# First mixture in groups of 4, 5 and 7 blocks: weight pace computed, odd partial sums on ScalarE and GpSimd, last Horner step in PSUM, scaled words in place

## The chip, the cores and the metric

The kernel runs on one core of a Trainium2 chip. Its metric is the time in microseconds (us) of one execution on the device, the median of several runs; lower is better. The core has five engines that run side by side and meet at semaphores: TensorE (PE in the profile; PEld is its weight load), VectorE (DVE), ScalarE (ACT), GpSimd (POOL) and SyncE (SP), which here only issues transfers. SBUF is the working memory, PSUM the small memory into which TensorE writes. GpSimd does not touch PSUM in this kernel.

## What is computed

Three stages run one after the other on 1536 tokens of width 512. The first is an attention with a mask by clusters, the second and the third are two wide layers ("mixtures"). The change is about the first mixture; the numbers below come from the reference, cut to this part.

```python
def _moe_ref(x, w_in, w_out, a, b):          # first mixture: d_model 512, d_ff 2048
    h = x @ w_in
    h2 = h * h
    h3 = h2 * h
    P = a[0] + a[1] * h + a[2] * h2 + a[3] * h3
    Q = 1.0 + np.abs(b[0]) * np.abs(h) + np.abs(b[1]) * h2
    g = P / (Q + 1e-06)
    return g @ w_out

def _moe2_ref(x, w_gate, w_val, w_out):      # second mixture: d_ff 1536
    g = x @ w_gate
    silu = g * (1.0 / (1.0 + np.exp(-g)))
    return (silu * (x @ w_val)) @ w_out
```

The weights reach the chip as 64-bit numbers. Each product is made from two float32 parts of every operand, a high and a low one, with three matmuls in place of one (high by high, high by low, low by high).

## The kernel before

**Tiles.** A mixture handles the tokens in three tiles `t` of 512 and the hidden width in blocks `f` of 128: 16 blocks in the first mixture, 12 in the second. One **unit** is a pair (t, f). For a unit of the first mixture, `first_half` lets TensorE make `h_ps` in a PSUM bank (12 matmuls, `product`, L600); the other engines turn it into `g`, high and low; and three loop turns later (`LH = 3`) `project` (L676) adds `g` times the block's output weights into the four PSUM banks of `acc` (12 matmuls more). Turn `n` of the loop at L733 gives TensorE the product of unit `n` and then the projection of unit `n - 3`. Four `h_ps` banks (`ps_h`) and four `acc` banks (`ps_a`) exist.

**The steps of a unit.** ScalarE writes `tq` and `tp` from `h_ps` (L617, L618). VectorE finishes the two polynomials: `tq` (L619), and Horner's steps for P on `tp` (L622, L623), all of which read `h_ps`. One turn later ScalarE makes the reciprocal `tr` (L628 to L630), VectorE the high part of g (L633), the product of g and Q (L636) and the rest (L639), and a further turn later GpSimd multiplies the rest by `tr` for the low part (L644). VectorE therefore has six instructions of 512 columns for each unit: L619, L622, L623, L633, L636, L639.

**Groups.** SBUF can't hold all 16 blocks with both their weights, so the blocks go in groups: for each group, all three token tiles, and for each tile all blocks of the group. In the first mixture the groups have 2, 4, 4, 3 and 3 blocks. When the last block of a group has been projected for a tile, `evac` empties the four banks: in the first group ScalarE copies them into the tile `part` (L688); in the later ones VectorE adds each bank to `part` (L694). After the last group `split_y` makes high and low parts of the sum for the second mixture (L707 on ScalarE, L708 on VectorE). In the second mixture the odd banks already go another way: ScalarE copies the bank to `ts` (L691) and GpSimd adds it to `part` (L692).

**Weights.** A block of weights arrives as `raw`, with 512 pairs of a low and a high 32-bit word in each partition, so the low and the high words lie at every second place. ScalarE scales the high words into the tile `u` (`block_shift`, L70). VectorE shifts `u` by three bits into `c` (L79) and adds the upper bits of the low words (L83); `c` is the weight as float32. ScalarE writes its high part (L91) and GpSimd its low part (L94) into one of 18 places. Two blocks belong to each `f` of the first mixture and three to each `f` of the second. The first nine blocks are converted during the attention; the others in the loop, by the list `until`, which spreads the blocks of the next group evenly over the turns of the current one.

**Order.** Nothing reorders the work: each engine runs its instructions as the code issues them. In a turn these are, past the matmuls: the sum of bank 0, the low part of g for the unit two turns back, the sum of bank 1, the polynomials of this unit, the sums of banks 2 and 3, the reciprocal of the unit before, `split_y`, the weight steps, and the quotient (L633 to L639) of the unit before.

## Time and profile before

| | us |
|---|---|
| median of 3 runs | 832.88 (832.59 to 833.62) |
| the profiled execution | 837.14 |
| its span in the trace | 835.4 |
| TensorE busy | 804.5 (96%) |
| VectorE busy | 614.6 (74%) |
| ScalarE busy | 449.8 (54%) |
| GpSimd busy | 311.7 (37%) |

The profiled execution is 4.26 us longer than the median, 0.5%. The attention lasts until about 250 us, the first mixture from there to about 527 us, the second until the end. Shares over the whole span mix these three; the rows below are therefore mostly of the first mixture. Matmuls overlap in the pipeline, so the length of one matmul says less than the time from one run of 12 to the next.

### The profile page before, as it was taken

How to read it: one execution, taken by the hardware profiler on the slowest of the kernel's cores; microseconds unless marked ns; L12 is line 12 of the kernel's file. 1: busy time of each engine (PE TensorE's matmuls, PEld its weight loads, DVE VectorE, ACT ScalarE, POOL GpSimd, SP SyncE). 2: the span in 40 equal slices, each digit the busy share in tenths (PEclk: the TensorE clock that was granted, in tenths of full speed). 3: DMA queues.
4: the chain of work that ended last, by engine and by line, in shares of the span. 5: the costliest groups of instructions: out<-in, count | busy, mean ns of one | idle time of the engine just before them, and what ended most of it. 6: DMA issues, size and time to landing. Idle time of an engine off the chain costs nothing.

```text
span 835.4 us, 11054 instructions
## 1 busy us (share of the span) xinstructions
PE 804.5 (96%) x3900; PEld 604.6 (72%) x3900; DVE 614.6 (74%) x929; ACT 449.8 (54%) x850; POOL 311.7 (37%) x274
## 2 busy tenths in 40 slices
PE   4999999999999999999998999999999999999997
PEld 3656566566557887778777777788888888888885
DVE  7777777687657999999999999974774655543344
ACT  5776776677766886766666567723432222221110
POOL 4565576477131343332343333321243332220121
PEclk8999999999999999999999999999999999999999
DMA  5265335533212212111121111112232212000003
GB/s 186 81 200 192 106 119 196 153 104 124 68 61 93 94 52 75 51 50 43 34 77 51 51 56 59 63 51 76 88 115 75 74 53 76 26 26 1 0 13 139
DMA packets 26551, 67.91 MB, mean 81 GB/s; under 512 B 4448, under 2 KB 9536, under 8 KB 26496
## 3 DMA queue, kind: packets, MB, share of 16 engines
q1 hardware_dynamic: 26496, 67.21, 24.5%
q8 instruction: 31, 0.51, 0.2%
q14 instruction: 24, 0.20, 0.1%
HBM read 59.48 MB, written 3.19 MB: 75 GB/s over the span
## 4 chain that ended last, share of the span: by engine, by line
PE 70%; DVE 22%; issue 3%; ACT 2%; DMA 1%; POOL 0%; DVEq 0%; POOLq 0%; ACTq 0%
PE h_ps L600 28%; PE acc L676 16%; PE o_ps L411 9%; PE t_ps L400 8%; PE s_ps L344 4%; PE s_ps L346 4%; DVE g L633 3%; DVE part L694 3%; DVE td L639 3%; DVE td L636 3%; DVE tq L619 2%; DVE tp L622 2%; DVE c L79 1%; DVE tp L623 1%; PE sim L277 1%
## 5 line engine op out<-in xcount | busy, mean ns | idle before, releaser
L600 PE MATMUL h_ps<-yhl,w 128*128 128x512 f32 x864 | 202.0, 389 | 0.0
L600 PEld LDWEIGHTS h_ps<-yhl,w 128*128 128x128 f32 x864 | 162.6, 188 | 33.9
L676 PE MATMUL acc<-g,w 128*128 128x512 f32 x576 | 146.2, 397 | 11.5 <-DVE part L694 6.8
L600 PE MATMUL h_ps<-xhl,w 128*128 128x512 f32 x576 | 138.7, 390 | 0.0
L676 PEld LDWEIGHTS acc<-g,w 128*128 128x128 f32 x576 | 106.9, 189 | 42.7 <-DVE part L694 10.7
L94 POOL TENSOR_TENSOR w<-c,w 128x512 fp32r<-128x512 f32 x68 | 93.1, 1371 | 109.7 <-ACT w L91 102.6
L600 PEld LDWEIGHTS h_ps<-xhl,w 128*128 128x128 f32 x576 | 107.9, 188 | 23.8 <-issue 1.2
L644 POOL TENSOR_TENSOR g<-td,tr 128x512 fp32r<-128x512 f32 x46 | 59.5, 1294 | 172.9 <-DVE td L639 146.9
L354 DVE TENSOR_REDUCE st<-s_ps 128x1 f32<-128x768 f32 x96 | 91.4, 953 | 30.5 <-PE s_ps L346 27.9
L405 ACT COPY pt<-t_ps 128x384 f32<-128x384 f32 x160 | 70.4, 483 | 64.6 <-PE t_ps L400 64.5
L694 DVE TENSOR_TENSOR part<-acc,part 128x512 f32<-128x512 f32 x74 | 48.6, 684 | 76.7 <-PE acc L676 76.6
L676 PE MATMUL acc<-w,g 128*128 128x512 f32 x432 | 103.3, 389 | 0.0
L400 PEld LDWEIGHTS t_ps<-ident,p 128*128 128x128 f32 x576 | 62.3, 142 | 54.6 <-issue 43.5
L676 PEld LDWEIGHTS acc<-w,g 128*128 128x128 f32 x432 | 81.1, 188 | 16.8
L362 ACT ACTIVATE p<-s_ps,st 128x768 f32<-128x768 f32 x96 | 87.6, 913 | 2.1 <-DVE st L354 1.2
L411 PE MATMUL o_ps<-pt,v 128*64 128x384 f32 x384 | 82.9, 514 | 2.0 <-DVE x L419 1.9
L400 PE MATMUL t_ps<-ident,p 128*128 128x128 f32 x576 | 84.7, 284 | 0.0
L691 ACT COPY ts<-acc 128x512 f32<-128x512 f32 x22 | 12.9, 588 | 111.5 <-PE acc L676 111.5
L692 POOL TENSOR_TENSOR part<-ts,part 128x512 f32<-128x512 f32 x22 | 30.2, 1393 | 111.9 <-ACT ts L691 111.9
L617 ACT ACTIVATE tq<-h_ps,babs 128x512 f32<-128x512 f32 x48 | 33.0, 688 | 68.7 <-PE h_ps L600 67.1
L344 PE MATMUL s_ps<-k,q 128*128 128x512 f32 x192 | 58.9, 388 | 1.8 <-ACT p L362 1.6
L661 ACT ACTIVATE sg<-h_ps 128x512 f32<-128x512 f32 x36 | 21.6, 601 | 67.6 <-PE h_ps L600 67.6
(101 smaller groups left out, 1075.6 us busy)
## 6 DMA issues: line engine op xcount, KB each, us to landing
raw<-w_in_dram SPq DMA_DIRECT2D x16, 512.0 KB
raw<-w_out_dram SPq DMA_DIRECT2D x16, 512.0 KB
raw<-w_gate_dram SPq DMA_DIRECT2D x12, 512.0 KB
raw<-w_val_dram SPq DMA_DIRECT2D x12, 512.0 KB
raw<-w_o_dram SPq DMA_DIRECT2D x12, 512.0 KB
xq<-q_t_dram SPq DMA_DIRECT2D x14, 384.0 KB
xk<-k_t_dram SPq DMA_DIRECT2D x14, 384.0 KB
sq<-q_s_dram SPq DMA_DIRECT2D x8, 384.0 KB
```

Of the source, the lines that this page charges most:

```text
L94: nc.gpsimd.tensor_tensor(out=w[:, 1, :], in0=t["c"], in1=r32(w[:, 0, :]), op=ALU.subtract)
L344: nc.tensor.matmul(s_ps[:, lo:hi], t["q1"][:, qs], t["k1"][:, lo:hi], start=True, stop=False)
L346: nc.tensor.matmul(s_ps[:, lo:hi], t["q2"][0:KM, qs], t["k2"][0:KM, lo:hi], start=False, stop=True)
L354: nc.vector.tensor_reduce(out=st[:, 0, k:k + 1], in_=live["s", b, hp, half, i, e], axis=AX.X, op=ALU.max, negate=True)
L362: nc.scalar.activation(out=p, in_=live.pop(("s", b, hp, half, i, e)), func=AF.Exp, bias=st[:, 0, k:k + 1], accum_out=st[:, 1, k:k + 1],)
L400: nc.tensor.transpose(t_ps[:, j, :], p[:, kb * P:(kb + 1) * P], ident)
L405: nc.scalar.copy(out=pt[:, ks, qc], in_=t_ps)
L411: nc.tensor.matmul(live["o", b, hp, half][e * D:(e + 1) * D, :], heads[b, 2 * hp + e]["v"][:, kb, :], live["pt", b, hp, half, e][:, kb, :] ...
L600: nc.tensor.matmul(h_ps, w[:, wi, cs], x[:, xi, cc, :], start=(n == 0), stop=(n == 3 * NCC - 1))
L644: spread.tensor_tensor(out=g[:, 1, :], in0=td, in1=tr, op=ALU.mult)
L676: nc.tensor.matmul(acc[c], lhs, rhs, start=(first and m == 0), stop=(last and m == 2))
L694: nc.vector.tensor_tensor(out=pt[:, c, :], in0=banks[c], in1=pt[:, c, :], op=ALU.add)
```

## The change

The diff, cut to what moves work:

```diff
     def block_shift(t):
-        t["u"] = pools["u"].tile([P, DM], F32, tag="u", name="u")
-        nc.scalar.activation(out=t["u"], in_=t["high"], func=AF.Prelu, scale=2.0**-112, alpha=2.0**32)
+        nc.scalar.activation(out=t["high"], in_=t["high"], func=AF.Prelu, scale=2.0**-112, alpha=2.0**32)
...
-        nc.vector.tensor_single_scalar(out=cb, in_=t["u"].bitcast(U32), scalar=3, op=ALU.logical_shift_left)
+        nc.vector.tensor_single_scalar(out=cb, in_=t["high"].bitcast(U32), scalar=3, op=ALU.logical_shift_left)
...
-    GROUPS = ((1, [2, 4, 4, 3, 3]), (2, [2, 2, 3, 3, 2]))
+    GROUPS = ((1, [4, 5, 7]), (2, [2, 2, 3, 3, 2]))
...
                 nc.vector.scalar_tensor_tensor(
-                    out=tp, in0=tp, scalar=coef[:, 1:2], in1=h_ps, op0=ALU.add, op1=ALU.mult
+                    out=h_ps, in0=tp, scalar=coef[:, 1:2], in1=h_ps, op0=ALU.add, op1=ALU.mult
                 )
...
-                    out=g[:, 0, :], in0=tp, scalar=coef[:, 0:1], in1=tr, op0=ALU.add, op1=ALU.mult
+                    out=g[:, 0, :], in0=h_ps, scalar=coef[:, 0:1], in1=tr, op0=ALU.add, op1=ALU.mult
...
-                    out=td, in0=tp, scalar=coef[:, 0:1], in1=td, op0=ALU.add, op1=ALU.subtract
+                    out=td, in0=h_ps, scalar=coef[:, 0:1], in1=td, op0=ALU.add, op1=ALU.subtract
...
-                elif layer == 2 and c % 2 == 1 and not (end and t == NTT - 1):
-                    ts = tmp_p.tile([P, T], F32, tag="ts", name="ts")
+                elif c % 2 == 1 and not (layer == 2 and end and t == NTT - 1):
+                    ts = tmp_p.tile([P, T], F32, tag="ts" if layer == 2 else "tl", name="ts")
                     nc.scalar.copy(out=ts, in_=banks[c])
                     nc.gpsimd.tensor_tensor(out=pt[:, c, :], in0=ts, in1=pt[:, c, :], op=ALU.add)
...
+        need = [used[key, f][0] - 2 for key, f, _ in loads]
+        free = [-1] * (WA + WX + WB) + [used[key, f][-1] + 1 for key, f, _ in loads]
+
+        pace = []
+        at = float(ready[0])
+        for n in range(len(seq)):
+            at += max(((b + 1 - at) / max(need[b] - n, 1) for b in range(int(at), len(loads))), default=0)
+            while free[min(int(at + 0.999), len(loads)) - 1] > n + 1:
+                at = int(at + 0.999) - 1
+            pace.append(min(int(at + 0.999), len(loads)))
...
-                want = c0 + -(-(c1 - c0) * (n + 1 - n0) // (n1 - n0))
+                want = pace[n]
```

The list `pace` says for each turn how many blocks shall be converted by then: fast enough that each is ready two turns ahead of its first use, and no faster than the 18 places come free. By the two lists, 3 blocks more are converted before the second mixture begins (32 after the first nine, where there were 29): two of them in turns 0 and 1, where there were none, and eight in turns 2 to 11, where there were seven. In turns 36 to 40 there are none, in turns 44 to 47 one in each. Fewer groups mean fewer ends of a group and tile in the first mixture: 9 where there were 15, so 36 sums of one bank where there were 60. Of these 36, 12 stay copies by ScalarE, 12 go to VectorE (48 before), and 12 take the way over ScalarE and GpSimd. The result of the third step of Horner's scheme stays in the `h_ps` bank until L638, one turn longer than the bank was held before. The copy `ts` takes a place of the tag "tl", which before held only `tp`. Past L66 the line numbers of the changed kernel are lower by one, as far as the steps named here are concerned.

What this moves, first on VectorE where a tile of a group ends in the middle of the first mixture. Before, a group of 4 blocks; the row L694 is a sum of one bank:

```order
L639 SCALAR_TENSOR_TENSOR td<-tp,coef,td 128x512
L694 TENSOR_TENSOR part<-acc,part 128x512 x2
L619 SCALAR_TENSOR_TENSOR tq<-tq,babs,h_ps 128x512
L622 TENSOR_TENSOR tp<-tp,h_ps 128x512
L623 SCALAR_TENSOR_TENSOR tp<-tp,coef,h_ps 128x512
L694 TENSOR_TENSOR part<-acc,part 128x512 x2
L79 TENSOR_SCALAR c<-u 128x512
L83 SCALAR_TENSOR_TENSOR c<-raw,c 128x512
L633 SCALAR_TENSOR_TENSOR g<-tp,coef,tr 128x512
```

And VectorE in the changed kernel at such an end (group of 5 blocks):

```order
L638 SCALAR_TENSOR_TENSOR td<-h_ps,coef,td 128x512
L693 TENSOR_TENSOR part<-acc,part 128x512
L618 SCALAR_TENSOR_TENSOR tq<-tq,babs,h_ps 128x512
L621 TENSOR_TENSOR tp<-tp,h_ps 128x512
L622 SCALAR_TENSOR_TENSOR h_ps<-tp,coef,h_ps 128x512
L693 TENSOR_TENSOR part<-acc,part 128x512
L78 TENSOR_SCALAR c<-raw 128x512
L82 SCALAR_TENSOR_TENSOR c<-raw,c 128x512
L632 SCALAR_TENSOR_TENSOR g<-h_ps,coef,tr 128x512
```

Two of the four sums have left VectorE here, one ahead of the polynomials and one behind them; the shift of the weights reads `raw` itself, and the quotient reads the PSUM bank.

ScalarE at such a place, before (L617 and L618 are the first steps of a unit, L628 to L630 the reciprocal of the unit before, L70 and L91 the weights):

```order
L617 ACTIVATE tq<-h_ps,babs 128x512
L618 ACTIVATE tp<-h_ps,coef 128x512
L628 ACTIVATE tq<-tq 128x512
L629 ACTIVATE tr<-tq,cbias 128x512
L630 ACTIVATE tr<-tr 128x512
L70 ACTIVATE u<-raw 128x512
```

And ScalarE in the changed kernel:

```order
L690 COPY ts<-acc 128x512
L616 ACTIVATE tq<-h_ps,babs 128x512
L617 ACTIVATE tp<-h_ps,coef 128x512
L690 COPY ts<-acc 128x512
L627 ACTIVATE tq<-tq 128x512
L628 ACTIVATE tr<-tq,cbias 128x512
L629 ACTIVATE tr<-tr 128x512
L69 ACTIVATE raw<-raw 128x512
L90 CAST w<-c 128x512
```

The copy of bank 1 now stands ahead of the unit's first step, and the copy of bank 3 ahead of the reciprocal of the unit before.

## Rows read from the trace of the kernel before

**Rows 1.** Stretches: length, busy us (count) of PE, PEld, DVE, ACT, POOL; clock; DMA.

```profile
460.00:500.00 40.00, 37.64 (x163) 29.84 (x162) 38.70 (x59) 25.58 (x41) 14.05 (x11) 1.00 0.16 54
...
580.00:620.00 40.00, 40.00 (x179) 33.10 (x178) 24.00 (x33) 15.44 (x28) 12.16 (x8) 1.00 0.24 79
```

**Rows 2.** Chain of work that ended last, by time: start us, us, what.

```profile
290.93 2.72 PE h_ps L600 x12
293.65 2.72 PE acc L676 x12
...
388.95 1.20 DVE part L694 x2
...
411.76 1.20 DVE part L694 x2
...
471.74 1.20 DVE part L694 x2
...
489.77 1.20 DVE part L694 x2
```

**Rows 3.** Timeline, TensorE, third product and first of second mixture: start us, us, what.

```profile
260.22 5.75 PE L600 MATMUL h_ps<-xhl,w 128*128 128x512 f32 x24
...
523.75 3.83 PE L676 MATMUL acc<-g,w 128*128 128x512 f32 x10 [1.78 <-POOL g L644]
...
527.37 5.97 PE L600 MATMUL h_ps<-yhl,w 128*128 128x512 f32 x24
```

**Rows 4.** Timeline, VectorE, one unit with a weight block.

```profile
355.85 0.74 DVE L619 SCALAR_TENSOR_TENSOR tq<-tq,babs,h_ps 128x512 f32<-128x512 f32 x1
...
357.88 0.42 DVE L79 TENSOR_SCALAR c<-u 128x512 uint32<-128x512 uint32 x1
...
358.95 0.75 DVE L633 SCALAR_TENSOR_TENSOR g<-tp,coef,tr 128x512 fp32r<-128x512 f32 x1
...
361.20 0.74 DVE L619 SCALAR_TENSOR_TENSOR tq<-tq,babs,h_ps 128x512 f32<-128x512 f32 x1
```

**Rows 5.** VectorE's groups by line, 250 to 530 us: count, busy us, mean ns.

```profile
L633 DVE SCALAR_TENSOR_TENSOR g<-tp,coef,tr 128x512 fp32r<-128x512 f32 x46 | 39.9, 867 | 1.5 <-ACT tr L630 1.5
...
L694 DVE TENSOR_TENSOR part<-acc,part 128x512 f32<-128x512 f32 x42 | 26.9, 683 | 0.0
...
L79 DVE TENSOR_SCALAR c<-u 128x512 uint32<-128x512 uint32 x29 | 17.2, 592 | 0.0
L708 DVE TENSOR_TENSOR yhl<-part,yhl 128x512 fp32r<-128x512 f32 x4 | 2.5, 686 | 0.0
```

**Rows 6.** One line's instructions, whole run: duration ns least/median/most, first and last start.

```profile
L633 DVE SCALAR_TENSOR_TENSOR g<-tp,coef,tr x48: 739/747/1315, 257.5 to 539.8; 128x512 fp32r<-128x512 f32 x48
L79 DVE TENSOR_SCALAR c<-u x68: 414/420/1053, 65.3 to 762.5; 128x512 uint32<-128x512 uint32 x68
L622 DVE TENSOR_TENSOR tp<-tp,h_ps x48: 679/680/685, 255.3 to 530.0; 128x512 f32<-128x512 f32 x48
L83 DVE SCALAR_TENSOR_TENSOR c<-raw,c x68: 680/693/1757, 68.8 to 762.9; 128x512 uint32<-128x512 uint32 x68
```

**Rows 7.** Timeline: GpSimd's low part of a weight block, and VectorE beside it.

```profile
362.70 1.29 POOL L94 TENSOR_TENSOR w<-c,w 128x512 fp32r<-128x512 f32 x1
...
363.25 1.30 DVE L633 SCALAR_TENSOR_TENSOR g<-tp,coef,tr 128x512 fp32r<-128x512 f32 x1
```

**Rows 8.** The page, costliest groups: the sum over two engines in the second mixture.

```profile
L691 ACT COPY ts<-acc 128x512 f32<-128x512 f32 x22 | 12.9, 588 | 111.5 <-PE acc L676 111.5
L692 POOL TENSOR_TENSOR part<-ts,part 128x512 f32<-128x512 f32 x22 | 30.2, 1393 | 111.9 <-ACT ts L691 111.9
```

**Rows 9.** Groups by line of the whole run: scaling of the high words.

```profile
L70 ACT ACTIVATE u<-raw 128x512 f32<-128x512 f32 x68 | 45.3, 666 | 13.3 <-DMA raw<-w_gate_dram 7.1 <-DMA raw<-w_out_dram 2.8 <-DMA raw<-w_in_dram 1.4
```

**Rows 10.** Timeline at the layer boundary: TensorE's second unit, VectorE's last quotient.

```profile
535.90 5.60 PE L600 MATMUL h_ps<-yhl,w 128*128 128x512 f32 x24
...
541.43 0.75 DVE L639 SCALAR_TENSOR_TENSOR td<-tp,coef,td 128x512 f32<-128x512 f32 x1
```

More of the change, by code (lines that the diff above doesn't have):

```diff
@@ L54, in stage_pools @@
     def stage_pools(stack, side, *bufs):
-        for name, n in zip(("raw", "u", "c"), bufs):
+        for name, n in zip(("raw", "c"), bufs):
             pools[name] = stack.enter_context(
@@ L128, in pool @@
         return stack.enter_context(tc.tile_pool(name=name, bufs=bufs, side=side, reuse_waits="tile", **kw))
-    stage_pools(A, "left", 1, 1, 1)
+    stage_pools(A, "left", 1, 1)
     base = pool(A, "base", 1, "left")
@@ L580, in tile_kernel @@
     with ExitStack() as mctx:
-        stage_pools(mctx, "right", 3, 2, 3)
+        stage_pools(mctx, "right", 3, 3)
         tmp_p = pool(mctx, "tmp_p", 3, "right")
@@ L710, in tile_kernel @@
         seq = []
-        until = []
-        total = 0
         for layer, sizes in GROUPS:
@@ L715, in tile_kernel @@
             for gi, gs in enumerate(sizes):
-                total += (layer + 1) * gs
-                until.append((len(seq), total))
                 for t in range(NTT):
@@ L721, in tile_kernel @@
                 f0 += gs
-        until.append((len(seq), total))
-        until[0] = (2, ready[0])
         LH = 3
-        gi = 0
+        used = {}
+        for n, (layer, t, f, *_) in enumerate(seq):
+            for key in "io" if layer == 1 else "gvp":
+                used.setdefault((key, f), []).append(n + LH * (key in "op"))
+        need = [used[key, f][0] - 2 for key, f, _ in loads]
[7 more added lines that the diff above has]
+            pace.append(min(int(at + 0.999), len(loads)))
         shifted, placed = [ready[0]], [ready[0]]
@@ L769, in tile_kernel @@
             if n < len(seq):
-                if n >= until[gi + 1][0]:
-                    gi += 1
-                (n0, c0), (n1, c1) = until[gi], until[gi + 1]
-                want = c0 + -(-(c1 - c0) * (n + 1 - n0) // (n1 - n0))
+                want = pace[n]
                 while len(started) < min(want + 2, len(loads)):
```

## The prediction

> **What bounds the kernel now.** I read the stretches first. In the second mixture TensorE has no free time (40.00 us of 40 busy, 179 matmuls) and VectorE is busy for 24.00; in the first mixture TensorE falls short (37.64 us, 163 matmuls) and VectorE is busy for 38.70 of 40, with ScalarE at 25.58 and GpSimd at 14.05 [rows 1]. So the first mixture is VectorE's, the second TensorE's, and only the first can give time back.
>
> How much? In the chain of waits, 12 matmuls follow 12 matmuls at 2.72 us, a product or a projection alike [rows 2]; a unit costs TensorE 5.44. From the third product (260.22 us) to the first product of the second mixture (527.37) lie 267.15 us [rows 3], and in them 46 products and 45 projections: 91 x 2.72 = 247.5. So 19.6 us are lost. The same by tiles: in the chain the sums on VectorE return after 22.81 us in a group of 4 blocks, where TensorE needs 21.76, and after 18.03 in a group of 3, where it needs 16.32 [rows 2]. Some of the 19.6 is clock: after a wait of 1.78 us for GpSimd's low part, 10 matmuls took 3.83 us [rows 3] in place of 2.27; there the granted clock was at the lower of its two levels for a while. **No change in the first mixture alone can bring more than about 19.9 us**, 19.6 and some 0.3 of slow matmuls just behind the mark (5.97 us for 24, and 5.75 elsewhere [rows 3]).
>
> What fills VectorE? A unit with a weight block and no disturbance takes 5.35 us from one L619 to the next, of which 1.07 are the block (L79 to L633) [rows 4]; so 4.28 for a unit. A sum costs 0.60 (two in 1.20 [rows 2]), a split of y 0.62 (2.5 for four [rows 5]). Between the two marks stand 46 units (196.9), 29 blocks (31.0), 42 sums (25.2) and 4 splits (2.5): 255.6. The rest to 267.15, 11.5 us, is VectorE held up by GpSimd: L633 takes 747 ns at its median and 867 on average, L79 420 and 592 [rows 5, 6], which makes 46 x 0.12 + 29 x 0.17 = 10.5; L83 has cases up to 1757 [rows 6]. The timeline shows one: GpSimd's L94 runs from 362.70 for 1.29 us, L633 starts 0.55 us into it and takes 1.30 [rows 7]. VectorE's list is as long as the stretch: it is the bound.
>
> **The change part by part**, on VectorE's list between the two marks.
>
> *Fewer and divided sums.* 42 become 10 (five tile ends of two; the last end lies behind the mark): 6.0 for 25.2, so -19.2.
>
> *Quotient from PSUM.* L633 read two SBUF tiles, its successor reads one SBUF tile and a PSUM bank. L622 reads such a pair and never takes more than 685 ns, beside the same GpSimd work [rows 6]; so the 46 x 0.12 = 5.5 of delay go. I expect some of it back, as 12 additions of about 1.3 to 1.4 us on GpSimd [rows 8] can hold up the instructions that still read two SBUF tiles (L636, L83): 0 to 3 us, by the 10.5 us that about 30 low parts cost now; I take 1. Together -4.5. The two further reads of a PSUM bank I cost at nothing, since L622 (680 ns) and L83 (two SBUF tiles, 693) [rows 6] differ by 13 ns.
>
> *Third Horner step into PSUM.* No row shows VectorE writing PSUM. Nearest are its reads: 680 to 693 ns with and without PSUM. I take 0, and 0.04 us either way a unit as bounds, 2 us each way in all; a far worse price is a rival below. Holding the bank longer costs nothing inside the mixture: product n+4 stands behind projection n, which needs GpSimd's low part of unit n, and that comes after the last read of the bank.
>
> *Scaled words in place.* The shift now reads every second word. L83 already reads the low words so and takes 693 [rows 6], so a step of two words alone is not slow, and I take L79's 420 on; the upper bound is L83's price, 0.27 x 32 = 8.6 less the holding-up that would then stop. ScalarE's L70 (666 ns [rows 9]) now writes every second word too, as it read before; nothing to half its time more, on an engine with 14 us free in 40 [rows 1].
>
> *Pace.* Three blocks more before the second mixture: +3.2. They stand in turns 0, 1 and 2 to 11, so VectorE enters the third unit some 2.5 us later. Eight splits rather than four lie inside: +2.5. The places for all blocks come free in time by the two lists, and the second mixture has room on VectorE for whatever is shifted.
>
> *Sum of the list*: -19.2 - 4.5 + 3.2 + 2.5 = -18.0, that is 249.1 for 267.15, while TensorE needs 247.5. **Neither engine is then clearly the bound; both are full to 99%**, and now their waits on each other count, which before were hidden in TensorE's idle time:
> - At a tile end ScalarE's copy of bank 1 stands ahead of the polynomials. It waits for the projection through bank 1 (1.36 us after the product) and takes 0.59 [rows 8], so VectorE's L619 can start some 1.9 us later than in other turns. Queued behind it are the reciprocal, the weights, and on VectorE everything. The slack in an ordinary turn: a unit's product ends at 2.72 us, two steps of ScalarE (some 0.7 each, after L691's 0.59) bring L619 to about 4.2, the 5.35 of VectorE's list to 9.5, GpSimd's 1.3 to 10.8; the projection asks for that low part (of the unit before) two turns and a product later with its third matmul, at 10.88 + 2.72 + 0.45 = 14.05. So about 3 us, and the 1.9 fit if nothing else is late. Six ends at 0 to 1 us: 2.5.
> - The last tile (blocks in turns 44 to 47, splits in turn 44) has 7 x 4.28 + 5 x 1.07 + 1.2 + 2.5 = 39.0 and about 1 us of delay for TensorE's 38.1: 0 to 3 us with the clock that a wait costs, taken as 1.5.
> - At the boundary each unit takes two `h_ps` banks. The second product of the second unit needs the bank that unit 47 now holds to its last quotient. Before, that product began at about 538.6 (535.90 + 2.72) and L639 of unit 47 at 541.43 [rows 10]. So up to 3.5 us; VectorE has no splits in that turn now and is less late: 1.
>
> That makes 5. VectorE's list is a lower bound, so the gain is 18.0 - 5 = **13.0 us**. Against the profiled execution: 837.14 - 13 = 824.1 with a span near 822.4; it lies 4.26 above the median, so the median should go from 832.88 to **819.9**.
>
> **The rivals.**
>
> *TensorE alone is the bound.* Waits cost little and GpSimd holds up VectorE less than I think; then 18 to 19.9 us are gained, 813 to 815. For it: a slack of 3 us, and 14 of 36 sums less on one engine. Against it: VectorE's list is 1.6 us over TensorE's even without any wait.
>
> *The words at every second place are slow.* L78 takes L83's price and with it the weight steps fill what the sums left: +8.6, less about 4 of delay that a slower form of reading might not meet, on the path since VectorE is full. 819.9 + 4.6 = 824.5; with none of that delay given back and 2.5 of waits more, 831. For it: 420 ns for 512 words is more than one a nanosecond, and no row has this form with such a source. Against it: L83.
> [...]
>
> *VectorE is slow into PSUM: slower than before.* The only instruction here that takes about double for the same 512 columns is GpSimd's L94 (1.29 us [rows 7], against 0.69). If L622 went to that, +0.6 x 46 = 28 us on the full engine, 848. It decides from 13 / 46 = 0.28 us a unit on. Against it: reads of PSUM cost nothing, and ScalarE's copy from a bank takes 588 ns [rows 8] like its other work.
>
> *The change doesn't do what it says.* If the sums were not the bound, nothing would move. The lists of instructions show 32 sums less, and the chain goes through them; small.
>
> **How the numbers follow.** Forecast (816 to 823): 0.55. TensorE alone (813 to 816): 0.13. Slow words, or more waits than counted (823 to 828): 0.18. The same at its upper end (828 to 831): 0.05. Nothing gained, within 0.2%, which is about what a measurement can tell from no change (831.2 to 834.5): 0.03. Slow PSUM (835 to 850): 0.06. The range 814 to 828 leaves out 0.14 above and some 0.04 below. Faster by over 0.2%: 0.91; the same 0.03; slower 0.06.
>
> **What would show it.** Right: L632's mean near 750 ns; L78 at a median of 420; L622 at 750; from the third product to the second mixture's first some 254 us; VectorE still over 95% busy there; waits of TensorE for L643 at tile ends and at the boundary, none longer than 3 us. Wrong: L78 at 690 (second rival), L622 above 1 us (third), VectorE with over 2 us free in 40 while TensorE has 40 of 40 (first), or TensorE waiting for L632 to L638 more often than before, which would mean that the latencies at tile ends were counted too low.

## The result, and the profile after

| | before | after |
|---|---|---|
| median of 4 runs, us | 832.74 (832.58 to 833.62) | 826.12 (824.47 to 826.76) |
| the profiled execution, us | 837.14 | 825.95 |
| its span, us | 835.4 | 824.2 |

The change takes 6.6 us off; the ratio is 0.991 [0.989, 0.993]. That is faster and half of the gain that was forecast. It lies inside the range, but in the interval 823 to 828, which had a chance of 0.18, and not in the one that was forecast (816 to 823). The profiled executions lie 11.2 us apart, but only 7.3 of that are in the first mixture: its third product begins 2.0 us earlier in the trace of after, and 1.9 come behind the second mark. I take the 2.0 as scatter: in the traces below that product begins between 257.7 and 261.2 us, early and late both with the change (258.2 here, 260.4 in bits_between) and without it (257.8 in horner_psum_alone). The cause of the 1.9 stays open. The medians decide; the traces tell where the 7.3 are.

The page of after, busy time of each engine:

```profile
PE 801.4 (97%) x3900; PEld 605.4 (73%) x3900; DVE 590.8 (72%) x893; ACT 454.4 (55%) x862; POOL 328.6 (40%) x286
```

TensorE's timeline of after, with the same two marks as [rows 3] and the one long wait between them (start us, us, what, in brackets the idle time before it and what ended it):

```profile
258.21 5.75 PE L599 MATMUL h_ps<-xhl,w 128*128 128x512 f32 x24
...
275.00 0.73 PE L675 MATMUL acc<-g,w 128*128 128x512 f32 x2 [0.16 <-DVE g L632]
277.87 3.99 PE L675 MATMUL acc<-g,w 128*128 128x512 f32 x10 [2.14 <-POOL g L643]
...
518.08 5.60 PE L599 MATMUL h_ps<-yhl,w 128*128 128x512 f32 x24
```

From mark to mark (from the first of these rows to the last) it is 259.87 us, where before took 267.15: TensorE still loses 12.4 us over its 247.5. Of these, 4.3 go in the turn around 275 us (9.73 us from one product to the next, for 5.44): a wait of 2.14 us and ten matmuls behind it at a lower granted clock (0.50 from 277.8 to 281 us), 3.99 us where ten take 2.56 at 1.00 (sums_dve, below).

The stretches of after, to set beside [rows 1] (length, busy us and count of PE, PEld, DVE, ACT, POOL; clock; DMA):

```profile
270.00:300.00 30.00, 27.70 (x115) 22.20 (x114) 27.27 (x41) 23.64 (x40) 11.59 (x9) 0.94 0.25 88
...
340.00:380.00 40.00, 38.42 (x170) 31.49 (x169) 38.63 (x54) 29.55 (x49) 19.20 (x15) 1.00 0.20 67
...
420.00:460.00 40.00, 39.12 (x170) 31.34 (x169) 38.52 (x56) 28.90 (x48) 18.15 (x16) 1.00 0.20 66
```

VectorE is still as full as in [rows 1] (38.6 of 40) from 340 to 460 us, though 30 sums have gone. Between the marks its busy time fell by 13.3 us only, from 257.41 to 244.15. The groups of VectorE show why. First before, between its marks (out<-in, count, busy us, mean ns, idle time before them and what ended it):

```profile
L633 DVE SCALAR_TENSOR_TENSOR g<-tp,coef,tr 128x512 fp32r<-128x512 f32 x45 | 39.2, 870 | 0.7 <-ACT tr L630 0.7
...
L636 DVE SCALAR_TENSOR_TENSOR td<-tq,g 128x512 f32<-128x512 f32 x45 | 33.1, 735 | 4.8
...
L83 DVE SCALAR_TENSOR_TENSOR c<-raw,c 128x512 uint32<-128x512 uint32 x29 | 21.2, 730 | 1.0
L79 DVE TENSOR_SCALAR c<-u 128x512 uint32<-128x512 uint32 x29 | 17.2, 592 | 0.0
```

and the same lines of after, between its marks, with the polynomials' L618:

```profile
L635 DVE SCALAR_TENSOR_TENSOR td<-tq,g 128x512 f32<-128x512 f32 x44 | 34.2, 778 | 4.3
L618 DVE SCALAR_TENSOR_TENSOR tq<-tq,babs,h_ps 128x512 f32<-128x512 f32 x46 | 34.1, 740 | 6.4 <-ACT tp L617 6.4
L632 DVE SCALAR_TENSOR_TENSOR g<-h_ps,coef,tr 128x512 fp32r<-128x512 f32 x45 | 33.5, 745 | 0.7 <-ACT tr L629 0.7
...
L82 DVE SCALAR_TENSOR_TENSOR c<-raw,c 128x512 uint32<-128x512 uint32 x31 | 23.5, 759 | 1.1
L78 DVE TENSOR_SCALAR c<-raw 128x512 uint32<-128x512 uint32 x31 | 21.5, 694 | 0.0
```

And the durations of after in the whole run (ns least/median/most), beside [rows 6]:

```profile
L78 DVE TENSOR_SCALAR c<-raw x68: 414/422/1510, 65.7 to 765.1; 128x512 uint32<-128x512 uint32 x68
L622 DVE SCALAR_TENSOR_TENSOR h_ps<-tp,coef,h_ps x48: 754/756/758, 254.0 to 521.4; 128x512 f32<-128x512 f32 x48
L632 DVE SCALAR_TENSOR_TENSOR g<-h_ps,coef,tr x48: 736/745/751, 255.4 to 529.5; 128x512 fp32r<-128x512 f32 x48
```

Read mean against median. L633 was held up by GpSimd (870 against 747); its successor L632 never is (at most 751). But L78 now takes 694 on average with an undisturbed time of 422, L82 759 and L635 778 with one of 693. Adding (mean - median) x count over VectorE's lines between the marks gives what I call its **hold-ups**: 13.5 us before, 14.3 after. They did not shrink; they moved. The second thing that is new is in the last column: VectorE waits 6.4 us for ScalarE's L617, where L619 waited for nothing. Most of that, 1.84, 1.06 and 1.06 us (at 287.85, 309.62 and 331.38), stands at the tile ends of the first group. ScalarE copies the banks there by L687, two of them ahead of the polynomials, as it did before; VectorE then came too late to notice. The first of the three:

```profile
285.29 1.27 ACT L687 COPY part<-acc 128x512 f32<-128x512 f32 x2 [5.52 <-PE acc L675]
...
287.85 0.75 DVE L618 SCALAR_TENSOR_TENSOR tq<-tq,babs,h_ps 128x512 f32<-128x512 f32 x1 [1.84 <-ACT tp L617]
```

The new copies (L690) come first at 356.69 us. Behind them VectorE waits at two of five ends, 0.17 and 1.51 us (at 387.65 and 495.54). The last 0.79 (at 482.81) are a wait for a product, with no copy ahead.

The 7.3 us are then: sums 25.6 to 6.8, -18.8; four more splits +2.5; two more blocks +2.2; 46 writes into PSUM at 8 ns more +0.4; hold-ups +0.8; together -12.9, against -13.3 measured; and waits for ScalarE from 0.7 to 7.1, +6.4. That makes -6.5; 0.8 us stay unassigned.

### The profile page after: what moved, and what is told of

Same layout as the page of the kernel before. It is cut to its first block, busy times and chain, and to the rows that moved or that the text cites. A ratio compares the mean times of both kernels' runs of the same rounds, so it can differ in the third digit from the quotient of the medians.

```text
span 824.2 us, 10986 instructions
## 1 busy us (share of the span) xinstructions
PE 801.4 (97%) x3900; PEld 605.4 (73%) x3900; DVE 590.8 (72%) x893; ACT 454.4 (55%) x862; POOL 328.6 (40%) x286
## 4 chain that ended last, share of the span: by engine, by line
PE 74%; DVE 18%; issue 2%; ACT 2%; POOL 1%; DMA 1%; DVEq 0%; POOLq 0%; ACTq 0%
PE h_ps L599 29%; PE acc L675 19%; PE t_ps L399 9%; PE o_ps L410 8%; PE s_ps L343 4%; PE s_ps L345 4%; DVE td L635 3%; DVE td L638 2%; DVE g L632 2%; DVE tq L618 2%; DVE tp L621 2%; DVE h_ps L622 2%; DVE c L78 2%; PE sim L276 1%; POOL g L643 1%
## 5 line engine op out<-in xcount | busy, mean ns | idle before, releaser
L675 PE MATMUL acc<-g,w 128*128 128x512 f32 x576 | 143.2, 395 | 7.1 <-POOL g L643 6.9
L93 POOL TENSOR_TENSOR w<-c,w 128x512 fp32r<-128x512 f32 x68 | 94.1, 1383 | 104.7 <-ACT w L90 103.9
L643 POOL TENSOR_TENSOR g<-td,tr 128x512 fp32r<-128x512 f32 x46 | 59.6, 1295 | 130.8 <-DVE td L638 119.2
L691 POOL TENSOR_TENSOR part<-ts,part 128x512 f32<-128x512 f32 x34 | 46.0, 1371 | 134.0 <-ACT ts L690 133.8
L690 ACT COPY ts<-acc 128x512 f32<-128x512 f32 x34 | 20.0, 590 | 142.6 <-PE acc L675 142.6
L693 DVE TENSOR_TENSOR part<-acc,part 128x512 f32<-128x512 f32 x38 | 26.0, 685 | 82.5 <-PE acc L675 82.4
L82 DVE SCALAR_TENSOR_TENSOR c<-raw,c 128x512 uint32<-128x512 uint32 x68 | 57.8, 849 | 2.0
L661 DVE TENSOR_TENSOR sg<-h_ps,sg 128x512 f32<-128x512 f32 x36 | 24.8, 688 | 41.0 <-ACT sg L660 40.1
```

Source lines behind the costliest of these rows:

```text
L82: nc.vector.scalar_tensor_tensor(out=cb, in0=t["low"].bitcast(U32), scalar=29, in1=cb, op0=ALU.logical_shift_right, op1=ALU.bitwise_or)
L93: nc.gpsimd.tensor_tensor(out=w[:, 1, :], in0=t["c"], in1=r32(w[:, 0, :]), op=ALU.subtract)
L643: spread.tensor_tensor(out=g[:, 1, :], in0=td, in1=tr, op=ALU.mult)
L675: nc.tensor.matmul(acc[c], lhs, rhs, start=(first and m == 0), stop=(last and m == 2))
L691: nc.gpsimd.tensor_tensor(out=pt[:, c, :], in0=ts, in1=pt[:, c, :], op=ALU.add)
```

## The experiments

Three theories stood for what was missing. **Hold-ups (H; "theory P" in the expectations)**: GpSimd's additions hold up VectorE's instructions that read SBUF twice or, like L78, take only 422 ns for 512 words, and the sums that were taken out had been the time in which those additions ran and harmed nobody. **Start (S)**: the blocks in turns 0 and 1 make VectorE late, which costs the 4.3 us around 275 us. **Late polynomials (L)**: ScalarE's copies ahead of L616 and L617 make VectorE wait at the tile ends. Runs are compared with before on the same chip, whose medians were 833.4 to 834.4. All numbers but the first two columns are between the marks of the profiled execution. That is one execution, and not always near the median: poly_first's took 822.9 us and that of orders_old_groups 822.5, each the fastest of its kernel, and groups_pace_alone's 836.2, so a column from the traces and a median can differ by some 3 us.

| kernel | median us | ratio | hold-ups | VectorE's waits for ScalarE | mark to mark | TensorE's loss |
|---|---|---|---|---|---|---|
| before | 832.7 | | 13.5 | 0.7 | 267.15 | 19.6 |
| after | 826.1 | 0.991 [0.989, 0.993] | 14.3 | 7.1 | 259.87 | 12.4 |
| groups_pace_alone | 833.5 | 0.9995 [0.9976, 1.0015] | 18.5 | 3.0 | 266.15 | 18.6 |
| horner_sums_undone | 833.8 | 1.0007 [0.9993, 1.0021] | 18.6 | 3.0 | 266.52 | 19.0 |
| sums_dve | 826.6 | 0.9909 [0.9881, 0.9937] | 9.9 | 4.1 | 259.03 | 11.5 |
| horner_psum_alone | 828.5 | 0.9944 [0.9923, 0.9966] | 7.3 | 1.5 | 261.70 | 14.2 |
| horner_sbuf | 840.3 | 1.0078 [1.005, 1.0107] | 23.3 | 11.3 | 273.59 | 26.1 |
| pace_turn2 | 826.8 | 0.9908 [0.9881, 0.9935] | 18.4 | 3.0 | 259.57 | 12.1 |
| bits_between | 823.0 | 0.9862 [0.9827, 0.9897] | 9.7 | 8.9 | 255.54 | 8.0 |
| poly_first | 825.7 | 0.9896 [0.987, 0.9921] | 13.0 | 5.0 | 257.28 | 9.8 |
| poly_first_bits | 819.3 | 0.9819 [0.98, 0.9839] | 10.5 | 5.4 | 252.40 | 4.9 |
| orders_old_groups | 825.0 | 0.9898 [0.9875, 0.9921] | 11.5 | 1.6 | 255.80 | 8.3 |
| orders_and_pace | 816.8 | 0.9797 [0.9778, 0.9815] | 8.8 | 4.1 | 248.97 | 1.5 |
| low_memset (one run) | 820.95 | | 0.3 | 9.8 | 250.42 | 2.9 |

### Which part of the change brings what

**horner_sbuf**: the changed kernel, with the third Horner step in SBUF as before.

```diff
-                    out=h_ps, in0=tp, scalar=coef[:, 1:2], in1=h_ps, op0=ALU.add, op1=ALU.mult
+                    out=tp, in0=tp, scalar=coef[:, 1:2], in1=h_ps, op0=ALU.add, op1=ALU.mult
...
-                    out=g[:, 0, :], in0=h_ps, scalar=coef[:, 0:1], in1=tr, op0=ALU.add, op1=ALU.mult
+                    out=g[:, 0, :], in0=tp, scalar=coef[:, 0:1], in1=tr, op0=ALU.add, op1=ALU.mult
...
-                    out=td, in0=h_ps, scalar=coef[:, 0:1], in1=td, op0=ALU.add, op1=ALU.subtract
+                    out=td, in0=tp, scalar=coef[:, 0:1], in1=td, op0=ALU.add, op1=ALU.subtract
```

> The changed kernel with the third Horner step written to SBUF again (L622, L632 and L638 as before). The forecast had 4.5 us for this part, since L632 no longer meets GpSimd: by it this run takes 829 to 831. Theory P: what GpSimd holds up only passes from one instruction to the next, so L632 goes from 745 to some 850 ns on average, L78, L82 and L635 fall by about as much together, and the time stays within 1.5 us of 826. By the third Horner step itself (756 ns into PSUM, 748 into SBUF) nothing is to be had.

It took 840.3 us, 14 more than after, more than before, and more than either expectation. VectorE's groups between the marks:

```profile
L632 DVE SCALAR_TENSOR_TENSOR g<-tp,coef,tr 128x512 fp32r<-128x512 f32 x45 | 38.4, 853 | 6.2 <-ACT tr L629 6.2
L638 DVE SCALAR_TENSOR_TENSOR td<-tp,coef,td 128x512 f32<-128x512 f32 x44 | 36.8, 835 | 1.5
```

and ScalarE's L617, what its idle time waited for (us, times):

```profile
  DVE td L638: 4.6, 3
```

L632 and L638 read two SBUF tiles again and are held up, 8.5 us for the two; 14.3 become 23.3. And there is a coupling that the prediction did not see: `tp` keeps its place of the tag "tl" until L638, the copies `ts` take places of the same tag, and ScalarE's L617 waits for a place. With the sums on VectorE the Horner end in SBUF costs 7.2 us (horner_sums_undone against sums_dve, below), with the way over ScalarE and GpSimd 14.2: the Horner end in PSUM is what makes that way affordable.

**sums_dve**: the changed kernel, with the odd sums back on VectorE.

```diff
-                elif c % 2 == 1 and not (layer == 2 and end and t == NTT - 1):
+                elif layer == 2 and c % 2 == 1 and not (end and t == NTT - 1):
```

> The changed kernel, but VectorE adds the odd banks of the first mixture too: 12 sums more on VectorE (0.60 us each, 7.2 us), and 12 copies of ScalarE and 12 additions of GpSimd less. If VectorE's list is what counts: 4 to 7 us more, 830 to 833. Theory L (ScalarE's copies ahead of the polynomials make VectorE wait, 6.4 us idle for L617 past the start): the idle time goes and most of it comes back, 825 to 828. Theory P: less GpSimd work, so L78, L82 and L635 are held up by some 3 us less in all, and the time is 828 to 830.

826.6 us, the same as after, as theory L had it. Ten sums more between the marks stand on VectorE (12.8 us for 6.8), and the stretch is 0.8 shorter rather than longer: hold-ups fell by 4.4 and waits for ScalarE by 3.0. Only 1.7 of the 3.0 are the waits behind L690. 1.4 fell at 287 us, ahead of any copy to `ts`, and go with the clock, whose mean from mark to mark is 1.00 here and 0.99 in after: TensorE waits as long in turn 5 as in after, but the ten matmuls behind it are not slow:

```profile
278.46 2.56 PE L675 MATMUL acc<-g,w 128*128 128x512 f32 x10 [2.13 <-POOL g L643]
```

**horner_sums_undone**: both edits together. What stays of the change is the groups, the pace and the words in place.

> The changed kernel with two parts undone: all later sums of the first mixture on VectorE, and the third Horner step in SBUF. To be read against the kernel with the sums alone undone (826.6 us, 259.0 us from the third product to the second mixture). With the sums on VectorE nothing else uses the places of tp, so this run has the Horner step's effect without theirs. Theory P (what GpSimd holds up passes to the next instruction): L632 rises to some 850 ns, L78, L82 and L635 fall by about the same sum, and the time is within 1.5 us of 826.6; the 14 us of the earlier run then came from the places of tp. If reading P from PSUM saves VectorE what the forecast said: 830 to 832.

**groups_pace_alone**: the kernel before, with the groups of 4, 5 and 7 and the list `pace` alone.

```diff
-    GROUPS = ((1, [2, 4, 4, 3, 3]), (2, [2, 2, 3, 3, 2]))
+    GROUPS = ((1, [4, 5, 7]), (2, [2, 2, 3, 3, 2]))
...
-                want = c0 + -(-(c1 - c0) * (n + 1 - n0) // (n1 - n0))
+                want = pace[n]
```

> The kernel before with the groups of 4, 5 and 7 and their pace alone; the 24 later sums stay on VectorE, the Horner end in SBUF, the scaled words in a tile of their own. VectorE has 24 sums less than before (14.4 us) and three blocks and four splits more (5.7). If the groups are what gains: 824 to 827, as the changed kernel. If Horner in PSUM is needed for it: 829 to 832.

Neither gains: 833.8 and 833.5, ratios 1.0007 and 0.9995. Both lie above what was expected of them. That hold-ups only pass from one instruction to the next, as theory P said, is wrong: horner_sums_undone has 18.6 us of them and sums_dve 9.9, and takes 7.2 us longer. So the words in place cost nothing, and **the groups and their pace, with 20 sums fewer between the marks (25.6 us of them down to 12.8), brought nothing**, where the prediction's terms for sums and pace would give some 7. VectorE's groups of groups_pace_alone, between the marks:

```profile
L633 DVE SCALAR_TENSOR_TENSOR g<-tp,coef,tr 128x512 fp32r<-128x512 f32 x45 | 37.3, 830 | 0.7 <-ACT tr L630 0.7
L639 DVE SCALAR_TENSOR_TENSOR td<-tp,coef,td 128x512 f32<-128x512 f32 x44 | 36.7, 835 | 1.5
...
L79 DVE TENSOR_SCALAR c<-u 128x512 uint32<-128x512 uint32 x31 | 20.4, 658 | 0.0
```

L639 took 752 on average before and takes 835 here, L79 658 for 592: hold-ups rise from 13.5 to 18.5. With the blocks and splits of the pace (+4.7) and the waits for ScalarE (+2.3) that eats 12.0 of the 12.8. The 4.7 had been forecast (as 5.7) and waits too (at other places); hold-ups that grow had not.

**horner_psum_alone**: the kernel before, with only the three Horner lines into PSUM.

> The kernel before with the Horner part of the change alone. The groups and the pace alone gave nothing (833.5), and with the groups, Horner in PSUM was worth 7.3 us (833.8 without, 826.6 with it, sums on VectorE). Theory P now says why: sums of VectorE read PSUM, so GpSimd works freely beside them; taking them away also takes this cover away, and the instructions that read SBUF alone are held up instead (L639 at 830 ns where it had 752). If so, Horner in PSUM gives back cover whatever the groups: L633 at 745 to 750, 4 to 7 us won, 826 to 829. If it is worth something only with fewer sums: 831 to 833.

828.5 us, 0.9944: 5 us, by hold-ups that fall from 13.5 to 7.3. Here "Quotient from PSUM" does what the prediction said of it, with all sums in place.

### Where a hold-up comes from

The timeline of before at a tile end, VectorE and GpSimd (start us, us, what):

```profile
342.58 0.75 DVE L639 SCALAR_TENSOR_TENSOR td<-tp,coef,td 128x512 f32<-128x512 f32 x1
343.25 1.28 DVE L694 TENSOR_TENSOR part<-acc,part 128x512 f32<-128x512 f32 x2
343.50 1.30 POOL L644 TENSOR_TENSOR g<-td,tr 128x512 fp32r<-128x512 f32 x1 [4.07 <-DVE td L639]
344.45 0.74 DVE L619 SCALAR_TENSOR_TENSOR tq<-tq,babs,h_ps 128x512 f32<-128x512 f32 x1
344.76 1.30 POOL L94 TENSOR_TENSOR w<-c,w 128x512 fp32r<-128x512 f32 x1
...
346.49 1.28 DVE L694 TENSOR_TENSOR part<-acc,part 128x512 f32<-128x512 f32 x2
...
347.68 0.42 DVE L79 TENSOR_SCALAR c<-u 128x512 uint32<-128x512 uint32 x1
```

and an ordinary turn of groups_pace_alone:

```profile
442.36 0.75 DVE L639 SCALAR_TENSOR_TENSOR td<-tp,coef,td 128x512 f32<-128x512 f32 x1
443.03 0.74 DVE L619 SCALAR_TENSOR_TENSOR tq<-tq,babs,h_ps 128x512 f32<-128x512 f32 x1
443.29 1.30 POOL L644 TENSOR_TENSOR g<-td,tr 128x512 fp32r<-128x512 f32 x1 [3.44 <-DVE td L639]
...
444.54 1.30 POOL L94 TENSOR_TENSOR w<-c,w 128x512 fp32r<-128x512 f32 x1
...
445.07 1.05 DVE L79 TENSOR_SCALAR c<-u 128x512 uint32<-128x512 uint32 x1
```

As soon as L639 ends, GpSimd runs two low parts one behind the other, some 2.6 us from L644's start. At the tile end of before VectorE spends them on L694, L619 and the two Horner steps, all of which have an operand in PSUM; GpSimd ends at 346.06, before the second pair of sums, and L79 takes its 0.42 us. In the ordinary turn there are only L619, L622 and L623, and L79 starts 0.53 us into L94: it takes 1.05 us and ends 0.28 after L94 does. Counted in the traces over all turns between the marks (a turn here from one L638 or L639 to the next), those with a low part of a weight block:

| kernel | four sums on VectorE: turns, hold-ups | two sums | none |
|---|---|---|---|
| before | 6, none | | 22, 21 (13.5 us) |
| groups_pace_alone | 3, none | | 25, 26 (18.6 us) |
| horner_psum_alone | 6, none | | 22, 11 (7.3 us) |
| sums_dve | 3, none | | 25, 15 (10.0 us) |
| after | | 3, 4 (3.8 us) | 25, 15 (10.4 us) |

So four sums cover the pair each time; two do not, with the two additions (L691) that GpSimd has there in place of the other sums. Of the 4.4 us by which sums_dve has less of hold-ups than after, 3.8 stand at these three ends. In groups_pace_alone the five hold-ups more make some 3 of the 5.0 by which the sum rises (there are three covered turns fewer and two blocks more); the rest is that each costs more, as L94 now meets L639 too.

The single instruction shows it too. In after 19 of L78, L82 and L635 are held up; 18 of them began while the weights' low part (L93) was running, and one L78 beside L691. The 18 end at a fixed time behind L93, L78 0.28 us, L82 and L635 0.55, whether they began 0.06 or 0.9 us into it. An L635 that begins 0.12 us ahead of L93 takes its 693 ns.

**low_memset** takes the suspected cause away: in the loop, GpSimd writes a constant in place of the weights' low part, and so reads nothing for it.

```diff
-                    block_lo(started[placed[0]], w)
+                    nc.gpsimd.memset(r32(w[:, 1, :]), 0.0)
```

> The changed kernel, in which GpSimd fills the low part of the weight blocks converted in the loop with zeros and reads nothing for it; the low parts of these weights are left out of the products. A probe of the hold-ups alone: if GpSimd's reading holds VectorE up, L82 falls to 700 ns or less on average (784 now) and L635 to 720 (772), the 12 us or so of hold-ups mostly go, and the stretch from the third product to the second mixture falls from 259.9 to 251 to 255 us. If VectorE's instructions are long for another reason (GpSimd's writing, the transfers, the strided words), L82 and L635 stay within 20 ns of what they were.

VectorE's groups between its marks:

```profile
L635 DVE SCALAR_TENSOR_TENSOR td<-tq,g 128x512 f32<-128x512 f32 x45 | 31.2, 693 | 4.7 <-DVE g L632 0.5
L82 DVE SCALAR_TENSOR_TENSOR c<-raw,c 128x512 uint32<-128x512 uint32 x31 | 21.5, 693 | 1.1
L78 DVE TENSOR_SCALAR c<-raw 128x512 uint32<-128x512 uint32 x31 | 13.3, 428 | 0.0
```

All three are back at their undisturbed times, hold-ups are 0.3, and the stretch is 250.42, 9.4 less than in after. It is one execution, of a kernel that also gives GpSimd other work, so the 9.4 are not the price of the hold-ups alone. That the weights' low part is the cause, and that L643 and the additions L691 alone do little harm in their places here, it does show. That the *reading* is, it does not: the constant takes GpSimd some 0.5 us (eight in 3.80, below) where L93 takes 1.35 in after, and between the marks it meets L78 and L635 only once each. The L635 took 693 ns, but the L78 took 667 (at 360.69 us, when the addition before it had ended). In the second mixture L78 meets it more often, and here one is held up for as long as GpSimd writes:

```profile
537.13 4.45 DVE L78 TENSOR_SCALAR c<-raw 128x512 uint32<-128x512 uint32 x1
...
537.51 3.80 POOL L786 MEMSET w<- 128x512 f32 x8
```

An addition (L691) is running when it begins and ends at 537.56; L78 ends 0.28 us behind the last of the eight writes. An L82 beside such a write took 694 ns.

None of VectorE's instructions with an operand in PSUM is long in after: L632 takes 751 ns at most, L618 751, L621 683, L622 758, L638 754 and the sums (L693) 692; one L632 (at 344.38 us) lies wholly beside L93 and takes 749. L635 and L82, with two inputs in SBUF and 693 ns undisturbed, reach 1780 and 1766 beside L93. L78, with one input in SBUF and 422 ns undisturbed, reaches 1510 beside L93, and 4454 beside writes alone (low_memset). That writes leave L635 and L82 alone rests on two cases (693 and 694 ns); why L78 is held up beside writes, no run shows.

### Order

**bits_between** gives the pair that is held up another place: L78 and L82 are issued between L635 and the last step of the quotient (L640 there), just ahead of the moment from which GpSimd runs.

```diff
-            def quotient():
+            def quotient(between=None):
...
+                if between:
+                    between()
                 nc.vector.scalar_tensor_tensor(
                     out=td, in0=h_ps, scalar=coef[:, 0:1], in1=td, op0=ALU.add, op1=ALU.subtract
```

> The changed kernel with one thing moved: VectorE's two weight steps (L78, L82) stand between L635 and L638 of the quotient, not ahead of it. [...] GpSimd's low parts of g and of a weight block follow each other for 2.6 us from the end of L638 on; behind it VectorE would now have L618, L621, L622, L632 (2.9 us, each with a PSUM operand) and only then L635, L78, L82. So P expects L78 near 450, L82 and L635 near 720, and 5 to 9 us less than the changed kernel: 817 to 821. Theory L (latency): what is left is lost because each step waits for the one before at the ends of tiles; the low part of g starts 1.1 us later here, so L expects the same or up to 4 us more: 826 to 830.

823.0 us, between the two expectations; the interval of its ratio touches that of after, but its hold-ups and its loss agree with the direction. Its timeline shows what GpSimd's pair now lies beside:

```profile
345.30 0.74 DVE L640 SCALAR_TENSOR_TENSOR td<-h_ps,coef,td 128x512 f32<-128x512 f32 x1
...
346.21 1.29 POOL L645 TENSOR_TENSOR g<-td,tr 128x512 fp32r<-128x512 f32 x1 [2.69 <-DVE td L640]
...
347.46 1.29 POOL L93 TENSOR_TENSOR w<-c,w 128x512 fp32r<-128x512 f32 x1
347.99 0.75 DVE L632 SCALAR_TENSOR_TENSOR g<-h_ps,coef,tr 128x512 fp32r<-128x512 f32 x1
348.85 0.69 DVE L635 SCALAR_TENSOR_TENSOR td<-tq,g 128x512 f32<-128x512 f32 x1
```

L618, L621, L622 and L632, all with PSUM, fill the time until 348.75, and L635 starts 0.1 us later, undisturbed. L82 stays at 693 throughout; L78 comes to 596 (450 was expected), and L635 does not fall to 720 but stays at 784, held up in the turns in which L93 meets it. Hold-ups fall to 9.7, the loss to 8.0.

**pace_turn2** tests S: no block in turns 0 and 1.

```diff
+            if n < 2:
+                pace.append(ready[0])
+                continue
```

> The changed kernel, but the pace converts no block in turns 0 and 1, as before. In the changed kernel TensorE lost 4.3 us in turn 5 (a wait of 2.14 us for GpSimd's low part, and 10 matmuls in 3.99 us behind it at the lower clock). Theory S (the early blocks delay VectorE and ScalarE by some 2.5 us at the start): the wait in turn 5 shrinks below 0.7 us and 2 to 4 us are won: 822 to 824. Theory P or a VectorE that is full throughout: the two blocks only move into later turns, the wait comes back there, and the time stays within 1.5 us of 826.

826.8 us, no gain. The turn around 275 us runs without loss, but the 4.3 us come back: hold-ups rise from 14.3 to 18.4 (L78 to 843), and TensorE's loss is 12.1, spread over 15 waits of 0.2 to 0.9 us. Where VectorE's list was still the bound, the wait that was removed only moved. In the changed kernel S is right about the wait and wrong about the gain.

**poly_first** tests L: ScalarE's polynomials are issued ahead of all copies and sums of a tile's end.

```diff
+            ahead = now if n < len(seq) and layer == 1 else None
+            if ahead:
+                ahead[0]()
             for e in ev[:1]:
                 e()
```

> The changed kernel with one order changed in the first mixture: the polynomials of a unit are issued ahead of all four sums of a tile's end, so that no copy of ScalarE stands ahead of L616 and no sum of VectorE ahead of L618. Theory L (the copies at tile ends make VectorE wait for L617: 6.4 us past the start): those waits go and 3 to 6 us are won, 820 to 823. Theory P alone: VectorE's list is as long as before and the time stays within 1.5 us of 826.

**poly_first_bits** has this order and that of bits_between.

> Both orders changed: the weight steps between L635 and L638, and the polynomials ahead of the sums. With the weight steps moved alone, 8.0 us were still lost between the marks, in single waits of TensorE for GpSimd's low part of 0.8 to 2.0 us, one at nearly each tile end. If these come from the copies ahead of the polynomials, they go: 2 to 4 us lost, 817 to 819 (a gain of 4 to 6 on the moved steps alone). If they come from GpSimd's own queue (the additions ahead of the low part), nothing changes: 822 to 824.

Alone the order brings 0.4 us in the median, within what can be told. VectorE's wait for L617 falls from 6.4 to 1.3, but the wait for the reciprocal (L629) rises from 0.7 to 3.7. On top of bits_between it brings 3.7 us (823.0 to 819.3, on two chips; the intervals of the ratios still overlap a little). The waits are the smaller part, and count only where the hold-ups don't fill the time that they leave.

**orders_and_pace** has both orders and the pace from turn 2 on; **orders_old_groups** is the same kernel with the old groups.

```diff
-    GROUPS = ((1, [4, 5, 7]), (2, [2, 2, 3, 3, 2]))
+    GROUPS = ((1, [2, 4, 4, 3, 3]), (2, [2, 2, 3, 3, 2]))
```

> The changed kernel with the weight steps between L635 and L638, the polynomials ahead of the sums, and no block in turns 0 and 1. With the two orders alone 4.9 us were still lost between the marks (819.3 us), 2.0 of them in turn 5. With room on VectorE the early blocks are no longer passed on to later turns, so now theory S should hold: the wait in turn 5 goes, 2.5 to 3.5 us stay lost, 817 to 818.5. If it comes back elsewhere as it did in the changed kernel: 819 to 820.

> As the run before (both orders, no block in turns 0 and 1), but with the old groups of 2, 4, 4, 3 and 3 blocks. Alone the new groups gave nothing. If they count once GpSimd holds little up, VectorE's 12 further sums (7.2 us), 12 further ones over ScalarE and GpSimd and six further tile ends cost 4 to 9 us: 822 to 827. If sums cost nothing because they are cover for GpSimd: within 1.5 us of the run with the new groups.

816.8 us, faster than both kernels: 2.0% below before and some 9 us below after. The stretches of orders_and_pace:

```profile
340.00:380.00 40.00, 40.00 (x178) 33.15 (x177) 38.77 (x59) 30.80 (x51) 19.72 (x16) 1.00 0.23 79
420.00:460.00 40.00, 40.00 (x178) 33.15 (x177) 38.69 (x58) 32.24 (x53) 18.37 (x14) 1.00 0.20 67
```

TensorE has 40.00 of 40 there, as in the second mixture [rows 1], and loses 1.5 us from mark to mark. The pace that did nothing in pace_turn2 is worth 2.5 us here (819.3 to 816.8 on different chips; 0.9819 and 0.9797, with intervals that overlap; from mark to mark 252.40 and 248.97). With the old groups the same orders take 825.0: now the groups are worth 8.2 us, which with their pace alone were worth none. It is not the sums alone: with the old groups this kernel has 10 sums more on VectorE between the marks, but also 4 blocks more and 4 splits less.

## Why the forecast was half right

**The bound, and what can be had.** Right: VectorE's list bounded the first mixture, and 19.6 us is what it could give back; the best kernel came to 1.5 of loss.

**Fewer and divided sums (-19.2).** The size was right, -18.8 between the marks (40 sums to 10; the 42 were counted up to 530 us). What failed was to book it whole as a gain: the sums were also the cover under which GpSimd worked. groups_pace_alone shows it: of 12.8 us of sums less, 4.7 went to the pace, 5.0 to new hold-ups and 2.3 to waits. And of the way over ScalarE and GpSimd itself nothing is left (sums_dve: 826.6 for 826.1), since the divided ends have 3.8 us of hold-ups, where ends with four sums have none, and the copies delay L617 (1.7 us).

**Quotient from PSUM (-4.5).** Here is the step that failed most, in its second half. The first, on L633, came as forecast, 870 to 745, and horner_psum_alone shows the whole term right as long as the sums stay (hold-ups 13.5 to 7.3). The "back" was taken as 1 us, from a bound of 0 to 3 that counted only the 12 additions on GpSimd. Measured, 6.3 us came back, on L78, L82 and L635 (hold-ups went from 13.5 to 14.3 while 5.5 of them left L633), 5.3 more than the term. The prediction's own working had the row for it: L79 was held up by 0.17 a block already [rows 5, 6], and it was kept at that; it went to 0.27. The additions themselves held up one L78 only (0.7 us). By the counts above, 3.8 us stand at the three ends where two sums had left VectorE, and 10.4 in 25 turns without sums, where horner_psum_alone has 7.3 in 22: what the prediction had missed is that the sums were cover.

**Third Horner step into PSUM (0, up to 2).** Right: L622 takes 756 for 748, 0.4 us in all. The third rival (slow writes, 848) is out. Unseen was what horner_sbuf shows, that this step also frees the places that `ts` needs.

**Scaled words in place (0).** Right: L78's median is 422 for 420, and horner_sums_undone and groups_pace_alone, which differ only by it, agree within their intervals. The second rival is out as a mechanism, though the time came out where it had put it (823 to 828) and its sign, L78 at 690, appeared in the mean: 694, by hold-ups and not by the words. The median told them apart. That a slower form would escape some 4 us of the delay, as the rival's sum has it, no run shows: L82, at 693 ns, was held up to 1766.

**Pace (+5.7).** The size was about right (+4.7 between the marks). "VectorE enters the third unit some 2.5 us later" was seen and not followed: it became the wait of 2.14 us in turn 5, with the lower clock (0.50) behind it 4.3. pace_turn2 shows that it was not the cause of the shortfall in this kernel.

**Waits (+5).** 6.4 by VectorE's rows, so 1.4 short, but that the sum came so near is luck. Where the prediction had put them, behind the new copies, stand 1.7; 4.0 stand at the ends of the first group, behind copies that were there before and that the prediction did not count, and 1.4 of these came with the lower clock. None at the end of a tile kept TensorE for more than 1.6 us. At the boundary, priced at 1, there is none: the second mixture's first two products follow each other in 8.16 us, as without a wait.

**TensorE alone (813 to 816)** is out for the changed kernel, and is about what orders_and_pace is.

In sum, 13.0 forecast and 7.3 measured between the marks: 5.3 by hold-ups that did not go (-4.5 forecast, +0.8 measured), 1.4 by waits, 0.4 by the sums, 0.4 by the writes into PSUM, and 1.0 the other way from the pace; 0.8 the other way stay open. The split rests on two traces, the cause of the hold-ups on the counts in five traces and on runs that move each part. VectorE was busy for 94% between the marks, where over 95 had been the sign of being right.

## What to carry to other kernels

Before an instruction is taken off a full engine, look at what runs on the other engines during it: here the sums, which GpSimd did not hold up (692 ns at most in before and after), were cover for its work, and of the 12.8 us of sums taken out in groups_pace_alone 5.0 went to new hold-ups. Compare mean and median of each line; a mean that rises while the median stays was a neighbour's doing here, and order helped more than less work. And where an engine is full, a wait that is taken away can come back elsewhere, as in pace_turn2: undo the cause of the fullness first, and then the same edit pays.

## What was not expected of the hardware

- A shift of 512 words a partition with a source at every second word kept its time: 422 ns for 420. ScalarE's write at every second word cost next to nothing either: L69 takes 666 ns at its median, L70 took 662 (666 on average [rows 9]).
- VectorE's third Horner step (L622) wrote a PSUM bank almost as fast as SBUF, 756 ns for 748.
- An instruction of VectorE that GpSimd held up lost up to 1.09 us in after: L78 took at most 1510 ns for 422, L635 1780 for 693. L78 was held up beside writes too, 4454 ns beside eight of them (low_memset).
- After a wait of TensorE of 2.14 us ten matmuls took 3.99 us, and the granted clock was 0.50 from 277.8 to 281 us, 0.94 on average from 270 to 300. In sums_dve ten took 2.56 after a wait of 2.13, at a granted clock of 1.00 on average from mark to mark; in horner_sbuf 3.63 after 1.82 (at 435.14; clock 0.96 from 420 to 460 us) and 2.56 after 1.80 (at 477.52; clock 1.00 from 460 to 500). In these runs the length of the wait alone does not tell whether the clock falls.
